# One spread stream of weight conversions in a fused attention and SwiGLU kernel

## The chip, the cores and the metric

The kernel runs on one core of one Trainium2 chip. The time is the device time of one execution in microseconds. A core has five engines that take their instructions in program order, each from its own queue, and wait for one another through semaphores: PE (TensorE, matrix multiply), DVE (VectorE), ACT (ScalarE), POOL (GpSimd) and SP, which here only issues DMAs. ACT issues DMAs too. PE writes to PSUM, which has eight banks of 2 KB a partition; other engines must empty a bank before PE can use it again.

## The reference

Rotary attention over 4 batches, 8 heads, 576 tokens and a head size of 64, and then a SwiGLU layer on the 2304 tokens of 512 values:

```python
attn = np.exp(scores - np.max(scores, axis=-1, keepdims=True))
attn = attn / (np.sum(attn, axis=-1, keepdims=True) + 1e-09)
x = np.matmul(attn, v).transpose(0, 2, 1, 3).reshape(2304, 512)
g = x @ w_gate                       # w_gate, w_val: 512 x 1536, w_out: 1536 x 512
silu = g * (1.0 / (1.0 + np.exp(-g)))
out = (silu * (x @ w_val) @ w_out).astype(np.float32)
```

Queries, keys and values are 32-bit floats; the weights come as 64-bit floats.

## The kernel before

Every 32-bit operand of a matmul is split into a high part `h` and a low part `l`, and a product is three matmuls: h·h, h·l, l·h. `split` makes the two parts: ACT casts the high part, and POOL or DVE subtracts it for the low one (both at line 674). A 64-bit weight is first made into a 32-bit one (`bits`, lines 720 to 726): a load of 512 KB into one of two `raw` buffers, one ACT operation (L720, the absolute value, "the sign bit" of the change), then six DVE operations (L721 to L726) of 128x512, in an `aux` PSUM bank.

The work after the attention has four stages. Tokens stand in two halves of 1152, each in three tiles of 384.

**Ordinary units** (`plain`): two blocks of 128 of the 1536 hidden columns are done as plain products, 2 blocks x 6 token tiles = 12 units u0 to u11 (`UNITS`) of 24 matmuls. `mm` writes to two of six PSUM banks; `ev` empties them on ACT (L766 Silu, L767 copy) and stores both results to DRAM, to `hf` for the first seven groups of 128 tokens (`FT = 7`) and to `ht` for the other eleven. So unit n+3 on PE waits for `ev` of unit n. Between the units stand: `xlate` (L662 to L666), which makes the second half's tokens ready, 4 chunks for each of two tiles (DVE add, DVE multiply, two ACT casts, DVE subtract, in sequence); `mix` and `forms2`, which make the token sums (T1, T0, T2) that the next stage multiplies; and the conversion of its first weights.

**Strassen passes**: the other ten blocks in ten passes s = 0 to 9 (gate and value in turn) through a seven-product scheme (`PROD`). A pass is three units q (token pairs p = 1, 2, 0), each of seven products of six matmuls. ACT copies the products k = 0 and 2 out of PSUM, DVE adds the five others, POOL makes two further sums after products 3 and 4 (L789). While pass s runs, `bits` converts the weights of pass s+2, `sums` (POOL) and two `split`s make the form `W0` or `W1` of pass s+1. The table `at(s, q, k, ...)` in `strassen` says after which product each of these stands in the program; `dq` is the list of conversion steps handed out after products. In gate passes ACT also applies Silu (L825) and issues the stores of the finished unit; in value passes SP issues them.

**First output part** (`finish`, first loop, `fdown`): for each of the 12 hidden blocks f, seven groups of 128 tokens times the output weights: 21 matmuls of 128x512. `fload` (SP) reads the block's gate and value, 896 KB, into one of two `HF` buffers, DVE multiplies them (L854), ACT casts `fh`, POOL subtracts `fl`; the output weight of block f+4 is converted (`obits`) and split (`Oh` on ACT, `Ol` on POOL).

**Second output part** (second loop, `down`): for the other eleven groups, 36 matmuls of 128x512 each.

All engines' order is the program's. Every DMA carries one of eight semaphores in turn, whichever queue issues it; a DMA whose semaphore is still held by an earlier one waits for that one's landing, and the instructions behind it in its queue wait too.

Of the kernel before, what the change touches and what calls it, by code (L numbers as in the profile page):

```python
# [52 lines left out]
    st=3,  # L53
# [461 lines left out]
FT = 7  # L515
# [3 lines left out]
class Moe:  # L519
# [50 lines left out]
    def open_early(self, ctx):  # L570
        def pool(name, bufs):
            return ctx.enter_context(self.tc.tile_pool(name=name, bufs=bufs, reuse_waits="tile", side="right"))
        one = pool("m_one", 1)
        self.Wb[1] = self.wbuf(one, 1)
        self.slot["raw0"] = pool("m_raw0", 1)
        self.s_p = pool("m_s", 3)
# [16 lines left out]
    def open_mid(self, ctx):  # L593
        def pool(name, bufs, **kw):
            return ctx.enter_context(self.tc.tile_pool(name=name, bufs=bufs, reuse_waits="tile", side="right", **kw))
        one = pool("m_mid", 1)
        self.wform(one, 1)
        self.own(one, "HF1", [128, 2, FT * 128], FP32)
        self.c_p = pool("m_cp", 2)
# [76 lines left out]
    def forms(self, p, c, Z, e, le):  # L676
# [8 lines left out]
        return ops, self.split(le, *(t[:, :, c] for t in self.T[p]), Z)  # L685
# [76 lines left out]
    def ev(self, f, s, t, ps):  # L762
        nc = self.nc
        sg = self.s_p.tile([128, BK], FP32, name="sv")
        v = self.s_p.tile([128, BK], FP32, name="sv")
# [5 lines left out]
    def keep(self, i, f, o, x, q):  # L771
        n = x.shape[-1]
        m = min(max(FT * 128 - o, 0), n)
        d = q.dma_start
        if m:
            d(out=self.hd[0][i, f, :, o:o + m], in_=x[:, 0:m])
        if m < n:
            t = (o + m) // 128 - FT
            d(out=self.hd[1][i, t:t + (n - m) // 128, :, f, :].rearrange("t p q -> p t q"),
              in_=x[:, m:n].rearrange("p (t q) -> p t q", q=128))  # L780
# [54 lines left out]
    def of(self, f):  # L835
        if not self.OF:
# [9 lines left out]
    def fload(self, f):  # L846
        if f < 2:
            self.HF.append(self.again(("WF1", "HF1")[f], [128, 2, FT * 128], FP32, "HF"))
        self.nc.sync.dma_start(out=self.HF[f % 2], in_=self.hd[0][:, f].rearrange("i p q -> p i q"))

    def fsplit(self, f):
        hh, hl = self.fs[f] = [self.again(f"xa{(f + 1) % 3}{x}", [128, FT * 128], F32R, f"f{x}") for x in "hl"]
        g, v = self.HF[f % 2][:, 0], self.HF[f % 2][:, 1]
# [30 lines left out]
    def hload(self, t):  # L884
        if t < FT + 2:
            self.HG[t % 2] = self.again(f"T0{'lh'[t % 2]}", [128, 2, NFF, 128], FP32, "hg")
        self.nc.sync.dma_start(out=self.HG[t % 2], in_=self.hd[1][:, t - FT].rearrange("i p f q -> p i f q"))

    def hsplit(self, t):
# [3 lines left out]
        for z in range(0, NFF, 3):  # L893
            g, v = (G[:, i, z:z + 3] for i in range(2))
# [46 lines left out]
def attn_swiglu(ctx: ExitStack, tc: tile.TileContext, qk, vr, wg, wv, wo, tab, out):  # L941
# [4 lines left out]
    hd = (dr.tile([2, NFF, 128, FT * 128], FP32, name="hf"), dr.tile([2, 18 - FT, 128, NFF, 128], FP32, name="ht"))  # L946
# [143 lines left out]
    jobs = plain(moe, ps)  # L1090
# [3 lines left out]
    strassen(moe, jobs)  # L1094
# [3 lines left out]
    finish(moe)  # L1098
# [15 lines left out]

def plain(moe, ps):
    nc = moe.nc
    ve, po = nc.vector, nc.gpsimd
    J = [Conv(moe, 1 + s // 2, s % 2, s % 2) for s in range(10)]
    st = {}
# [5 lines left out]
    for half in range(2):  # L1125
        J[0].load(half)
    moe.yload(1)
    moe.rload(1, 1)
    moe.yload(2)
    moe.rload(1, 2, moe.R12)  # L1130
    for c in range(2):
        mix(1, c, moe.Z2[:, c])
    for u, x in enumerate(UNITS):
# [4 lines left out]
        if u < 2:  # L1138
            run(J[0].bits(u, ve))
            J[1].load(u)  # L1140
        elif u < 6:
            for c in range(2):
                moe.xlate(2 * u % 4 + c, u // 2)
        if u == 1:
            run(J[0].sums(po))
        if u in (2, 3):
            run(st[1, u - 2])
        if u == 3:
            run(J[0].split(0, po))
        if u == 4:  # L1150
            run(J[0].split(1, po))
        if u == 5:
            moe.tagain(2)
            ops, st[2] = moe.forms2(po, ve)
            run(ops)
        if u == 6:
            run(J[1].bits(0, ve))
            J[2].load(0)
        if u == 7:
            run(st[2])  # L1160
            moe.tagain(0)
            mix(0, 0, moe.again("raw0", [128, 4, BK], FP32, "Z"))
            mix(0, 1, moe.rz())
        if u == 8:
            run(J[1].bits(1, ve))
            J[2].load(1)
        if u == 10:
            run(st[0, 0])
        if u == 11:
            run(st[0, 1])  # L1170
    return J
# [5 lines left out]
def strassen(moe, J):  # L1177
# [3 lines left out]

    def bits(s):
        ops = []
        for h in range(2):
            ops += J[s + 2].bits(h, ve) if s < 8 else moe.obits(2 * (s - 8) + h)
            ops.append((lambda h=h: J[s + 3].load(h)) if s < 7 else (lambda h=h: moe.oload(2 * (s - 7) + h)))
        return ops
# [4 lines left out]
    for s in range(9):  # L1192
# [5 lines left out]
        at(s, 0, 4, lambda s=s: run(J[s + 1].sums(po)))  # L1198
        at(s, 1, 2, hi)
        at(s, 1, 4, lo[0])  # L1200
        at(s, 2, 4, lo[1])
# [5 lines left out]
    for s in range(10):  # L1207
        fp, i = 1 + s // 2, s % 2
        dq = bits(s)
# [7 lines left out]
    for f in (2, 3):  # L1217
# [3 lines left out]
def finish(moe):  # L1221
    for f in range(NFF):
        if f + 2 < NFF:
# [46 lines left out]
```

## Time and profile before

| | us |
|---|---|
| three runs: lowest, median, highest | 787.62, 792.21, 792.47 |
| the profiled execution | 788.58 |
| its span, first to last instruction | 786.8 |

| busy in the span | PE | DVE | ACT | POOL |
|---|---|---|---|---|
| us | 719.0 | 552.9 | 406.1 | 469.5 |

Busy time is a mean over stages of different kinds, so each stage is read by itself: what PE waits for in it, and what stood on the chain of work that ended last. Starts are in us from the beginning of the span. PEclk is the clock granted to PE, 1.00 being the full 2.4 GHz.

### The profile page before, as it was taken

How to read it: one execution, taken by the hardware profiler on the slowest of the kernel's cores; microseconds unless marked ns; L12 is line 12 of the kernel's file. 1: busy time of each engine (PE TensorE's matmuls, PEld its weight loads, DVE VectorE, ACT ScalarE, POOL GpSimd, SP SyncE). 2: the span in 40 equal slices, each digit the busy share in tenths (PEclk: the TensorE clock that was granted, in tenths of full speed). 3: DMA queues.
4: the chain of work that ended last, by engine and by line, in shares of the span. 5: the costliest groups of instructions: out<-in, count | busy, mean ns of one | idle time of the engine just before them, and what ended most of it. 6: DMA issues, size and time to landing. Idle time of an engine off the chain costs nothing.

```text
span 786.8 us, 12626 instructions
## 1 busy us (share of the span) xinstructions
PE 719.0 (91%) x4356; PEld 670.1 (85%) x4356; DVE 552.9 (70%) x891; ACT 406.1 (52%) x878; POOL 469.5 (60%) x466
## 2 busy tenths in 40 slices
PE   7799999999999999686989899898998977899997
PEld 6699999999999989586889899898998855678887
DVE  4899888888888885565757566575656877745541
ACT  2689888888988863443531434314343223243331
POOL 5796989999899578369456464564655745400000
PEclk9999999999999999789889999999999999999999
DMA  5888698888888957924343454534447756676761
GB/s 150 219 205 219 180 249 219 217 217 219 210 211 215 226 172 179 226 69 134 93 148 113 129 151 134 170 108 135 147 134 238 250 201 222 253 264 213 228 218 41
DMA packets 103824, 144.11 MB, mean 183 GB/s; under 512 B 17728, under 2 KB 75088, under 8 KB 103760
## 3 DMA queue, kind: packets, MB, share of 16 engines
q1 hardware_dynamic: 77968, 125.71, 55.6%
q10 hardware_dynamic: 25792, 17.59, 7.3%
q8 instruction: 35, 0.57, 0.3%
q14 instruction: 29, 0.24, 0.1%
HBM read 76.61 MB, written 42.54 MB: 151 GB/s over the span
## 4 chain that ended last, share of the span: by engine, by line
PE 57%; POOL 11%; DVE 10%; DMA 8%; ACT 7%; issue 6%; ACTq 1%; SPq 1%; POOLq 0%; DVEq 0%
PE ch L801 18%; PE ch L908 12%; PE pv L476 9%; PE sc L360 8%; PE tr L436 6%; POOL fl L674 2%; DVE nmt L375 2%; DMA hf<-sv 2%; POOL W1l L674 1%; PE tr L299 1%; PE ch L758 1%; POOL Z L680 1%; POOL W0l L674 1%; ACT E L393 1%; POOL R L680 1%
## 5 line engine op out<-in xcount | busy, mean ns | idle before, releaser
L375 DVE TENSOR_REDUCE nmt<-sc 128x1 f32<-128x576 f32 x144 | 107.8, 750 | 21.1 <-PE sc L360 19.8
L393 ACT ACTIVATE E<-sc,nmt 128x576 f32<-128x576 f32 x128 | 97.2, 759 | 9.5 <-DVE nmt L375 8.6
L789 POOL TENSOR_TENSOR u<-u,z 128x384 f32<-128x384 f32 x30 | 30.4, 1014 | 102.7 <-DVE sg L789 88.5
L436 PE MATMUL tr<-ident,E 128*128 128x128 f32 x512 | 77.2, 274 | 0.6 <-DVE N L322 0.6
L360 PE MATMUL sc<-QK 128*128 128x288 f32 x248 | 61.5, 329 | 3.4 <-DMA QK<-N 2.0
L436 PEld LDWEIGHTS tr<-ident,E 128*128 128x128 f32 x512 | 61.6, 141 | 2.5 <-PE tr L299 1.3
L224 POOL TENSOR_TENSOR t<-X,tabs 128x256 f32<-128x256 f32 (+1 forms) x90 | 51.8, 596 | 15.5 <-DVE rot L228 6.8
L804 ACT COPY c<-ch 128x384 f32<-128x384 f32 x30 | 14.4, 479 | 78.1 <-PE ch L801 78.1
L360 PE MATMUL sc<-N,QZ 128*128 128x288 f32 x248 | 53.6, 298 | 1.1 <-DMA QZ<-N 1.1
L908 PE MATMUL ch<-Oh,hh 128*128 128x512 f32 (+1 forms) x144 | 54.0, 375 | 0.1
L908 PE MATMUL ch<-Oh,hl 128*128 128x512 f32 (+1 forms) x144 | 53.9, 374 | 0.0
L908 PE MATMUL ch<-Ol,hh 128*128 128x512 f32 (+1 forms) x144 | 53.8, 374 | 0.0
L437 ACT CAST ET2h<-tr 128x512 fp32r<-128x512 f32 x80 | 47.0, 587 | 12.5 <-PE tr L436 12.5
L438 DVE TENSOR_TENSOR ET2l<-tr,ET2h 128x512 fp32r<-128x512 f32 x80 | 52.9, 681 | 0.5 <-ACT ET2h L437 0.5
L721 DVE TENSOR_SCALAR aux<-aux 128x512 f32<-128x512 f32 x32 | 22.3, 696 | 40.8 <-ACT aux L720 40.6
L228 POOL TENSOR_TENSOR rot<-rot,t 128x512 f32<-128x512 f32 (+1 forms) x45 | 45.7, 1016 | 3.5
L789 DVE TENSOR_TENSOR sg<-ch,u 128x384 f32<-128x384 f32 x60 | 33.3, 554 | 19.8 <-PE ch L801 19.3
L438 DVE TENSOR_TENSOR ET1l<-tr,ET1h 128x512 fp32r<-128x512 f32 x64 | 42.7, 684 | 6.3 <-ACT ET1h L437 6.2
L674 ACT CAST hh<-hg 128x384 fp32r<-128x384 f32 x44 | 22.6, 514 | 47.1 <-DVE hg L895 46.3
L674 DVE TENSOR_TENSOR hl<-hg,hh 128x384 fp32r<-128x384 f32 x44 | 25.8, 587 | 29.8 <-ACT hh L674 29.8
L437 ACT CAST ET1h<-tr 128x512 fp32r<-128x512 f32 x64 | 36.4, 597 | 18.0 <-PE tr L436 14.8
L227 POOL TENSOR_TENSOR rot<-X,tabs 128x512 f32<-128x512 f32 (+1 forms) x45 | 45.6, 1014 | 0.0
(400 smaller groups left out, 2463.9 us busy)
## 6 DMA issues: line engine op xcount, KB each, us to landing
QK<-N SPq DMA_DIRECT2D x62, 288.0 KB, 4.8
hg<-ht SPq DMA_DIRECT2D x11, 1536.0 KB, 7.8
HF<-hf SPq DMA_DIRECT2D x12, 896.0 KB, 5.6
X<-in_qk_dram SPq DMA_DIRECT2D x15, 576.0 KB, 6.5
yd<-Y SPq DMA_DIRECT2D x31, 256.0 KB, 3.8
Xab<-yd SPq DMA_DIRECT2D x32, 192.0 KB, 6.1
raw<-in_moe_w_out_dram SPq DMA_DIRECT2D x12, 512.0 KB, 3.4
raw<-in_moe_w_gate_dram SPq DMA_DIRECT2D x11, 512.0 KB, 4.1
```

What stands on the lines that cost most here:

```text
L224: ins = e.tensor_tensor(out=sel(t2, u), in0=sel(x, w), in1=tb(Sn, u), op=ALU.mult)
L360: nc.tensor.matmul(ps[:, g, 0:288], l, rr[:, o + g * 288:o + (g + 1) * 288], start=(x == 0), stop=(x == len(terms) - 1))
L375: nc.vector.tensor_reduce(out=nmcol, in_=ps[:, :, 0:288], axis=AX.XY, op=ALU.max, negate=True)
L393: nc.scalar.activation(out=E.rearrange("p (a b) -> p a b", a=2), in_=ps[:, :, 0:288], func=ACTF.Exp, bias=nmcol, scale=1.0, accum_out=self ...
L436: nc.tensor.transpose(ps[:, c], E[:, o + c * 128:o + (c + 1) * 128], self.ident)
L437: nc.scalar.copy(dst[0], src)
L438: nc.vector.tensor_tensor(out=dst[1], in0=src, in1=r32(dst[0]), op=ALU.subtract)
L476: nc.tensor.matmul(st["ps"][:, 0:w], VS[:, sl, :], t, start=(x == 0), stop=(x == last))
L674: return [lambda: self.nc.scalar.copy(h, f), lambda: le.tensor_tensor(out=l, in0=f, in1=r32(h), op=ALU.subtract)]
L789: add = lambda e, out, in0, in1: e.tensor_tensor(out=out, in0=in0, in1=in1, op=ALU.add)
L801: nc.tensor.matmul(acc, l[:, w, c * 128:(c + 1) * 128], r[:, c], start=(n == 0), stop=(n == 5))
L908: self.nc.tensor.matmul(ps, l[:, f], r[:, z], start=(n == 0), stop=(n == 3 * NFF - 1))
```

## The change

The conversions become one list of jobs (`Stream`): the 20 halves of gate and value weights and the 12 output weights, in the order of their use, with the output weights 4, 5 and 6 put in after the weights of passes 4, 6 and 8 (into a new buffer `OX`). `take(n)` gives the steps of n jobs; after the fourth of a job's six DVE steps it puts the ACT operation of the **next** job (`sign`), and after the last one the load of the job after that (`load`). A pass takes one to three jobs and spreads their steps evenly over its 21 products. In `finish` the five output weights that are left (7 to 11) are converted in iterations 0 to 4, each with `sign` at the start of its iteration.

In the passes, `split` of the next pass moves up: the casts from after product (1, 2) to (1, 0), the two subtractions from (1, 4) and (2, 4) to (1, 1) and (1, 4), written as (unit, product).

In `plain`, four jobs are converted in the first four units in place of two; `xlate` moves from u2 to u5 to u4 to u7; the second token tile's loads move behind u1; `forms2` runs on DVE and not on POOL; the T0 sums start at u3 on POOL.

The DRAM buffers hold gate and value side by side: `hf` as [f, 128, 7, 2, 128] and `ht` as [t, 128, f, 2, 128]. So an ordinary unit is one store (two where the border between `hf` and `ht` runs through it) in place of two or four, `fload` and `hload` read one piece per partition of twice the length, and a Strassen store to `hf` writes pieces of 512 bytes where it wrote up to 3 KB. All Strassen stores are issued by SP.

```diff
+class Stream:
+    def take(self, n, ahead=True):
+        out = []
+        for x in range(n):
+            for k in range(6):
+                out.append(lambda k=k: self.ops[0][k]())
+                if k == 3 and (ahead or x + 1 < n):
+                    out.append(self.sign)
+            out.append(lambda: self.ops.pop(0))
+            out.append(self.load)
+        return out
...
     def ev(self, f, s, t, ps):
-        nc.scalar.activation(out=sg, in_=ps[0], func=ACTF.Silu)
-        nc.scalar.copy(v, ps[1])
-        for i, x in enumerate((sg, v)):
-            self.keep(i, f, s * SG + t * BK, x, nc.scalar)
+        sv = self.ld_p.tile([128, 2, BK], FP32, name="Xab").rearrange("p a q -> p (a q)")
...
+        self.keep(f, 9 * s + 3 * t, sv.rearrange("p t i q -> p t (i q)"), slice(0, 2), nc.scalar)
...
-            self.keep(i, 2 * fp + j, 2 * p * BK, sg[j].rearrange("p j q -> p (j q)"), (self.nc.scalar, self.nc.sync)[i])
+            self.keep(2 * fp + j, 6 * p, sg[j].rearrange("p j (t q) -> p (j t) q", q=128), slice(i, i + 1), self.nc.sync)
...
     for u, x in enumerate(UNITS):
-        if u < 2:
-            run(J[0].bits(u, ve))
-            J[1].load(u)
-        elif u < 6:
-            for c in range(2):
-                moe.xlate(2 * u % 4 + c, u // 2)
+        if u < 4:
+            run(S.take(1, u < 3))
         if u == 1:
             run(J[0].sums(po))
+            moe.yload(2)
+            moe.rload(1, 2, moe.R12)
+        if 4 <= u < 8:
+            for c in range(2):
+                moe.xlate(2 * u % 4 + c, u // 2 - 1)
...
-            ops, st[2] = moe.forms2(po, ve)
+            ops, st[2] = moe.forms2(ve, ve)
...
-        at(s, 1, 2, hi)
-        at(s, 1, 4, lo[0])
-        at(s, 2, 4, lo[1])
+        at(s, 1, 0, hi)
+        at(s, 1, 1, lo[0])
+        at(s, 1, 4, lo[1])
...
-                run(dq, {0: 2, 2: 2, 5: 1}.get(k, 0))
-        run(dq)
+                g += 1
+                run(dq, g * m // 21 - (m - len(dq)))
...
     for f in range(NFF):
+        if S.begun < len(S.jobs):
+            S.sign()
...
+        if S.ops:
+            run(S.take(1, False))
         if f + 4 < NFF:
-            run(moe.obits(f + 4))
             run(moe.osplit(f + 4))
-            if f + 6 < NFF:
-                moe.oload(f + 6)
         moe.fdown(f)
```

POOL in pass 0, before. The `u` and `sg` rows are the sums after products 3 and 4 of the units q = 0, 1, 2; `W1l` are the two low parts of the weights of pass 1.

```order
L789 TENSOR_TENSOR u<-u,z_5000 128x384
L789 TENSOR_TENSOR sg<-sg,z_5000 128x384
L928 TENSOR_TENSOR WF_4442<-WF_4442 128x256
L929 TENSOR_TENSOR WF_4442<-WF_4442 128x256
L930 TENSOR_TENSOR WF_4442<-WF_4442 128x256
L931 TENSOR_TENSOR WF_4442<-WF_4442 128x256
L789 TENSOR_TENSOR u<-u,z_5072 128x384
L789 TENSOR_TENSOR sg<-sg,z_5072 128x384
L674 TENSOR_TENSOR W1l<-WF_4442,W1h 128x1024
L789 TENSOR_TENSOR u<-u,z_5150 128x384
L789 TENSOR_TENSOR sg<-sg,z_5150 128x384
L674 TENSOR_TENSOR W1l<-WF_4442,W1h 128x1024
```

The same place in the change (the four `sums` of this one pass stand earlier, in the ordinary units).

```order
L786 TENSOR_TENSOR u<-u,z_4985 128x384
L786 TENSOR_TENSOR sg<-sg,z_4985 128x384
L674 TENSOR_TENSOR W1l<-WF_4439,W1h 128x1024
L786 TENSOR_TENSOR u<-u,z_5051 128x384
L786 TENSOR_TENSOR sg<-sg,z_5051 128x384
L674 TENSOR_TENSOR W1l<-WF_4439,W1h 128x1024
L786 TENSOR_TENSOR u<-u,z_5128 128x384
L786 TENSOR_TENSOR sg<-sg,z_5128 128x384
```

Both low parts stand one unit, seven products, earlier: the second one behind the sums of q = 1, not of q = 2.

ACT in the ordinary units u2 and u3, before: `sv` are the results, `xa2h` and `T0h` what `xlate` makes.

```order
L720 ACTIVATE aux<-raw 128x512
L766 ACTIVATE sv<-ch 128x384
L767 COPY sv<-ch 128x384
L776 DMA hf<-sv 128x128
L779 DMA ht<-sv 128x2x128
L776 DMA hf<-sv 128x128
L779 DMA ht<-sv 128x2x128
L664 CAST xa2h<-aux 128x384
L665 COPY T0h<-aux 128x384
L664 CAST xa2h<-aux 128x384
L665 COPY T0h<-aux 128x384
L674 CAST T1h<-T0l 128x4x384
```

The same place in the change; the two L720 rows are those of the third and the fourth job, and `Xab` is the buffer of the results.

```order
L720 ACTIVATE aux<-raw 128x512
L766 ACTIVATE Xab<-ch 128x3x128
L767 COPY Xab<-ch 128x3x128
L774 DMA hf<-Xab 128x256
L777 DMA ht<-Xab 128x2x256
L720 ACTIVATE aux<-raw 128x512
L674 CAST T1h<-T0l 128x4x384
```

Two of four stores and the four casts of `xlate` have left this place, and the absolute value of the third job now stands ahead of the Silu of u2, that of the fourth ahead of the Silu of u3.

ACT in `finish`, before: `fh` belongs to block f+2, L720 and `Oh` to the output weight f+4.

```order
L674 CAST fh<-HF 128x896
L720 ACTIVATE aux<-raw 128x512
L674 CAST Oh<-OF 128x512
L674 CAST fh<-HF 128x896
L720 ACTIVATE aux<-raw 128x512
```

The same place in the change, iterations 0 to 1 and 4 to 5:

```order
L720 ACTIVATE aux<-raw 128x512
L674 CAST fh<-HF 128x896
L674 CAST Oh<-OX 128x512
L720 ACTIVATE aux<-raw 128x512
L674 CAST fh<-HF 128x896
L674 CAST Oh<-OX 128x512
...
L674 CAST fh<-HF 128x896
L674 CAST Oh<-OF 128x512
L674 CAST fh<-HF 128x896
L674 CAST Oh<-OF 128x512
```

L720 comes first in its iteration and belongs to a weight that is split three iterations later; from iteration 5 on there is none. `Oh` takes a weight that was converted in an earlier iteration or pass.

## Rows read from the trace of the kernel before

**Rows 1.** Stretch, us, busy of PE PEld DVE ACT POOL, PEclk, DMA, GB/s
```profile
289.00:360.60 71.60, 60.62 (x314) 58.36 (x313) 43.97 (x61) 29.66 (x54) 46.51 (x33) 0.90 0.60 155
360.60:615.30 254.70, 229.11 (x1252) 225.09 (x1251) 161.57 (x274) 87.18 (x136) 143.56 (x125) 0.95 0.46 142
615.30:691.00 75.70, 63.54 (x264) 47.78 (x262) 55.71 (x72) 23.19 (x35) 39.86 (x23) 1.00 0.60 221
```
**Rows 2.** What PE waited for, 280 to 361 us: total, times, longest
```profile
PE ch L758 <- ACT sv L766: 10.7, 5, 4.0
```
**Rows 3.** The same, 361 to 616 us
```profile
PE ch L801 <- POOL W1l L674: 15.3, 5, 3.2
...
PE ch L801 <- POOL W0l L674: 2.4, 4, 0.6
```
**Rows 4.** The same, 615 to 691 us
```profile
PE ch L864 <- POOL fl L674: 11.1, 8, 1.4
```
**Rows 5.** The chain that ended last, in pass 0: start, us, what
```profile
394.50 0.96 POOL sg L789
395.46 2.31 POOL W1l L674
```
**Rows 6.** PE in order of time: two matmuls 92 apart, pass 9
```profile
600.83 0.34 PE L801 MATMUL ch<-xa1h,W1l 128*128 128x384 f32 x1
...
616.78 0.34 PE L801 MATMUL ch<-xb0l,W1h 128*128 128x384 f32 x1
```
**Rows 7.** The chain that ended last: the second output part
```profile
691.00 91.79 PE ch L908 x432
```
**Rows 8.** The chain that ended last, in the first output part
```profile
620.08 8.10 DMA HF<-hf
...
658.70 2.04 POOL fl L674
```
**Rows 9.** DVE in order, first output part; in brackets idle before
```profile
638.38 0.70 DVE L721 TENSOR_SCALAR aux<-aux 128x512 f32<-128x512 f32 x1 [1.58 <-ACT aux L720]
...
642.64 1.08 DVE L854 TENSOR_TENSOR HF<-HF 128x896 f32<-128x896 f32 x1
```
**Rows 10.** DMA issues 640 to 672 us: count, KB, us to landing
```profile
HF<-hf SPq DMA_DIRECT2D x5, 896.0 KB, 5.4
```
**Rows 11.** DMA issues 380 to 600 us
```profile
raw<-in_moe_w_val_dram SPq DMA_DIRECT2D x8, 512.0 KB, 3.4
```
**Rows 12.** DMA issues 300 to 330 us
```profile
raw<-in_moe_w_val_dram SPq DMA_DIRECT2D x2, 512.0 KB, 7.5
```
**Rows 13.** As rows 1: the loaded part of the ordinary units
```profile
303.00:330.00 27.00, 22.68 (x114) 22.04 (x112) 16.16 (x24) 7.92 (x17) 16.14 (x15) 0.87 1.09 265
```
**Rows 14.** ACT in order of time, ordinary units
```profile
322.25 0.49 ACT L767 COPY sv<-ch 128x384 f32<-128x384 f32 x1
325.25 1.50 ACTq L776 DMA_DIRECT2D hf<-sv  x2
```
**Rows 15.** DVE in order of time, ordinary units
```profile
316.35 0.57 DVE L663 TENSOR_TENSOR aux<-aux,R 128x384 f32<-128x384 f32 x1 [3.61 <-DMA R<-rd]
...
333.30 2.73 DVE L662 TENSOR_TENSOR aux<-T0h,T2h 128x384 f32<-128x384 f32 x1
...
338.03 0.56 DVE L662 TENSOR_TENSOR aux<-T0h,T2h 128x384 f32<-128x384 f32 x1
...
340.59 0.55 DVE L662 TENSOR_TENSOR aux<-T0h,T2h 128x384 f32<-128x384 f32 x1
```
**Rows 16.** POOL in order of time, at the second row of rows 15
```profile
332.61 3.00 POOL L674 TENSOR_TENSOR W0l<-WF,W0h 128x1024 fp32r<-128x1024 f32 x1 [12.92 <-ACT W0h L674]
```
**Rows 17.** PE in order: first matmul of pass 0's second unit
```profile
377.60 0.69 PE L801 MATMUL ch<-xa2h,W0h 128*128 128x384 f32 x1 [0.19 <-DVE u L789]
```
**Rows 18.** DVE's groups in the passes, by shape: busy us, mean ns
```profile
L789 DVE TENSOR_TENSOR sg<-ch,u 128x384 f32<-128x384 f32 x59 | 32.7, 555 | 19.8 <-PE ch L801 19.3
...
L725 DVE SCALAR_TENSOR_TENSOR aux<-raw,aux 128x512 f32<-128x512 uint32 x21 | 14.5, 691 | 0.4
```

More of the change, by code (lines that the diff above doesn't have):

```diff
@@ L597, in open_mid @@
         self.wform(one, 1)
-        self.own(one, "HF1", [128, 2, FT * 128], FP32)
+        self.own(one, "HF1", [128, FT, 2, 128], FP32)
+        self.OX = self.own(one, "OX", [128, NX, DM], FP32)
         self.c_p = pool("m_cp", 2)
@@ L1089, in attn_swiglu @@
     moe.open_aux(xctx, 2)
-    jobs = plain(moe, ps)
+    J, S = plain(moe, ps)
     mctx.close()
@@ L1093, in attn_swiglu @@
     moe.open_mid(mctx)
-    strassen(moe, jobs)
+    strassen(moe, J, S)
     xctx.close()
@@ L1112, with __init__, load, sign @@
          (0, 1, 1), (1, 1, 1), (0, 1, 2), (1, 1, 2)]
+class Stream:
+    def __init__(self, moe, jobs):
+        self.jobs = jobs
+        self.ops, self.loaded, self.begun, self.done = [], 0, 0, 0
+    def load(self):
+        if self.loaded < len(self.jobs):
+            self.jobs[self.loaded][0]()
+            self.loaded += 1
+    def sign(self):
+        if self.begun < len(self.jobs):
+            ops = self.jobs[self.begun][1]()
+            self.begun += 1
+            ops[0]()
+            self.ops.append(ops[1:])
+    def take(self, n, ahead=True):
[8 more added lines that the diff above has]
+        return out
 def plain(moe, ps):
@@ L1118, in plain, with job @@
     J = [Conv(moe, 1 + s // 2, s % 2, s % 2) for s in range(10)]
+    jobs = []
+    def job(kind, x, h=0):
+        if kind == "w":
+            jobs.append((lambda: J[x].load(h), lambda: J[x].bits(h, ve)))
+        else:
+            jobs.append((lambda: moe.oload(x), lambda: moe.obits(x)))
+    for s in range(10):
+        for h in range(2):
+            job("w", s, h)
+        if s in (4, 6, 8):
+            job("o", 2 + s // 2)
+    for f in (0, 1, 2, 3, 7, 8, 9, 10, 11):
+        job("o", f)
+    S = Stream(moe, jobs)
     st = {}
@@ L1123, in mix @@
         run(ops)
-    for half in range(2):
-        J[0].load(half)
+    S.load()
+    S.load()
     moe.yload(1)
     moe.rload(1, 1)
-    moe.yload(2)
-    moe.rload(1, 2, moe.R12)
+    S.sign()
     for c in range(2):
@@ L1149, in plain, with strassen @@
             run(J[0].split(0, po))
+            mix(0, 0, moe.again("raw0", [128, 4, BK], FP32, "Z"))
         if u == 4:
             run(J[0].split(1, po))
+        if 4 <= u < 8:
+            for c in range(2):
+                moe.xlate(2 * u % 4 + c, u // 2 - 1)
         if u == 5:
+            mix(0, 1, moe.rz())
+        if u == 7:
             moe.tagain(2)
-            ops, st[2] = moe.forms2(po, ve)
+            ops, st[2] = moe.forms2(ve, ve)
             run(ops)
[L1156 to L1159, printed above, removed]
+            run(J[1].sums(po))
+        if u == 8:
             run(st[2])
             moe.tagain(0)
[L1162 to L1166, printed above, removed]
+        if u in (9, 10):
+            run(moe.split(ve, *(t[:, :, u - 9] for t in moe.T[0]), st[0, u - 9]))
         if u == 10:
[L1168 to L1171, printed above, removed]
+            S.sign()
+            run(S.take(1))
+    return J, S
 ORDER = (1, 2, 0)
-def strassen(moe, J):
+def strassen(moe, J, S):
     nc = moe.nc
@@ L1208, in strassen @@
         fp, i = 1 + s // 2, s % 2
-        dq = bits(s)
+        n = {0: 1, 2: 3, 4: 3, 6: 3}.get(s, 2)
+        dq = S.take(n, s < 9)
+        m, g = len(dq), 0
         for q, p in enumerate(ORDER):
```

57 lines of the change are left out of this document (27 added, 30 removed).

## The prediction

> **What bounds the kernel now.** I read the page's share of busy time first, then the busy time by stretch, the PE waits of each stretch, the chain that ended last, and single engines in order of time where a wait stood out. PE is busy 719.0 of 786.8 us, so only its waits and its clock can be won. The attention's order is the same on every engine, and PE's order is the same everywhere: the matmuls stay. The second output part is bare PE: 432 matmuls in 91.79 us with no other engine in the chain [rows 7]; counted by width they are 396 full 512-column ones, 0.2318 us each. Nothing there moves. Three stretches remain, 289.0 to 360.6, 360.6 to 615.3 and 615.3 to 691.0 [rows 1]:
>
> - Ordinary units: PE waits 10.7 us for `sv`, in five waits, the longest 4.0 [rows 2].
> - Passes: 15.3 us for `W1l` in five waits and 2.4 for `W0l` in four [rows 3], at a granted clock of 0.95 [rows 1].
> - First output part: 11.1 us for `fl` in eight waits [rows 4], at full clock.
>
> The sum is made against the profiled execution's own 788.58 us. That lies 3.6 below the median of the three runs (792.21) and near the lowest (787.62).
>
> **Passes: −25 us (bounds −28 and −15).** 92 matmuls of pass 9 take 616.78 − 600.83 = 15.95 us, 0.1734 each, with no wait between [rows 6]. From the second unit of pass 0, at 377.60 [rows 17], to the first output part at 617.1 (the last row of [rows 6] and its 0.34) there are 29 units of 42 = 1218 matmuls: 211.2 us bare, 239.5 measured, 28.3 lost. 17.7 of these are the waits of [rows 3]; the other 10.6 is time at the lower of the two clock levels (1.2, not 2.4 GHz), which the stretch's 0.95 shows and which follows the long waits.
>
> In a gate pass the second `W1l` stands on POOL behind the sums of the unit q = 2: sum until 395.46, then the low part, 2.31 us, and PE wants it at once [rows 5]. So each wait is one such operation (15.3 / 5 = 3.1 with its surroundings). The change puts it seven products earlier: 42 × 0.1734 = 7.3 us, against a wait of 3.1, leaves 4 us. The casts ahead of it move too, to (1, 0); the first low part then waits for them and for POOL's `sums` of up to 2 us behind (0, 4), inside the same margin. The `W0l` waits of 0.6 go the same way. No wait, no fall of the clock: I book 25 of 28.3.
>
> What the even stream costs: before, a pass had two jobs; now it has one to three, 22 in all. In one with three, DVE has 15 evictions × 0.555 + 18 conversion operations × 0.691 [rows 18] = 20.8 us, against a pass of 126 × 0.1734 = 21.9. DVE is at 95% in three passes, 76% in the others (12 operations, 16.6 us). Six PSUM banks cover a late eviction by some 5 us. ACT's absolute value now stands between the copies of products and waits for a raw load that was issued half a job earlier: 21.9 / 3 / 2 = 3.65 us in the three-job passes, 5.5 in the others, where before's load landed after 3.4 [rows 11]; between ends of 3.4 and 7.5 (under heavy traffic, [rows 12]) I take 3.4, since the stretch moves 142 GB/s, not 265 [rows 1, 13]. 7.5 would make ACT 3.9 us late per job, under the banks' 5. If a third of the waits came back so, the term would be −15. The stores that leave ACT for SP cost nothing on PE: SP only waits.
>
> **First output part: −9 us (bounds −12 and −5).** 12 blocks of 21 matmuls are 252 × 0.2318 = 58.4 us; measured are 691.0 − 617.1 = 73.9. In every iteration DVE stands 1.58 us waiting for ACT's L720 and then does seven operations; the next L721 comes 645.30 − 638.38 = 6.92 us after the last one (the first is [rows 9]; six such periods follow alike), and `Ol` and `fl` (2.04, [rows 8]) come behind it. The change issues L720 at the iteration's start, so the 1.58 goes, and five iterations convert where eight did. What is then late, block by block from 617.1: block 3 still waits for its `HF` load, which took 8.10 us to 628.2 [rows 8]; multiply 1.08, cast 0.95, `fl` 2.04 and hand-overs put it at +16. Blocks 4 to 7 follow DVE: six operations at 0.73 (with the 0.03 between) and the multiply of 1.08, up to 1.6 with strided operands, 5.9 each: block 7 starts at +39.6. From there the two `HF` buffers are the limit: load 5.4 [rows 10], multiply, cast, `fl` and hand-over 4.8, 10.2 per two blocks, 5.1 each, against PE's 4.87. Four such blocks and the last block's 4.87: +64.9. The gain is 9.0. With PE bare after block 3 it would be +59.8 and some hand-overs, −12; with the `HF` loads at the 8.10 of the first one, 6.45 per block from block 7, −5.
>
> **Ordinary units: −2 us (bounds −9 and +4).** Moved here: four jobs in four units, `xlate` two units later, `forms2` to DVE, T0 earlier. For: before, DVE stood 3.61 us until 316.3 for an `R` load [rows 15], with casts ahead of the Silu on ACT; that goes. Against: the transfers run at 265 GB/s with all DMA engines busy (share 1.09, [rows 13]), so order decides. The raw load of the fourth job (0.52 MB, 2.0 us) now stands in the same train, lands near 316.8, and its absolute value stands ahead of a Silu: a new wait of some 3.5 us near u5, and the longest wait of before, 4.0, shrinks for it. The `T2` load then lands behind two raw loads, near 327.7 where before a store issue stood until 325.25 behind it (the copy ahead of it had ended at 322.74, [rows 14]). That store's 1.5 us and the Silu and copy behind it reach 331 to 332; eight `xlate` chunks at 340.59 − 338.03 = 2.56 us [rows 15] add 20.5, to 352.5; four DVE operations of `forms2` of about 0.9, a cast and a low part follow, 7 us: the passes start at 359.5, 1.1 sooner. Pass 0's first unit held 377.60 − 360.6 − 7.3 = 9.7 us of waits; with POOL freed of `forms2` and `sums` 3.5 of it go: second unit at 373, −4.6.
>
> The cover that could fail is shown by one row: L662 at 333.30 took 2.73 us where its likes take 0.56 [rows 15], and POOL's `W0l` ran from 332.61 for 3.00 [rows 16]; both ended within 0.5 us. Now all eight L662 and four `forms2` operations run beside POOL's long chain. I take half of the gain, 375.5, between 373 and the 378 to 380 of twelve late operations. Taken beyond these, −9 is most of the 10.7 of `sv` waits gone, and +4 the twelve operations all late (13 us) with two thirds of it covered or regained.
>
> The Trainium skill (page "SBUF — State Buffer", section "SBUF: two separate sides") says that DVE and GpSimd share one port pair as an exclusive lock held for the whole instruction, and that a DVE operation with two SBUF inputs against a GpSimd one that reads SBUF is such a case. By that rule every L662 and `forms2` operation that meets a running POOL operation waits to its end, and the term is about +2, not −2. The row at 333.30 agrees with it; the rows here do not show whether those of 0.56 met a POOL operation.
>
> **The sum.** −25 − 9 − 2 = −36: 752.6 as a profile, 754 as a median, some 1.4 above, since the three runs lie from 1 below to 4 above the profile.
>
> **Rivals.**
> - *DVE is held by POOL in all of the ordinary units.* Twelve operations lose half of 2.2 us each, some 13 on the chain, half of it covered by PE's units: the term is +2 in place of −2, and POOL's own low parts come late, so that one `W1l` wait of 3 stays: 754 + 4 + 3 = 761 (758 to 768). For it: the one row. Against: 338.03 and 340.59 run at 0.56.
> - *Raw loads come late in the passes.* SP now has all stores and loads of a pass in one line; if a load lands 6 to 7 us after issue, ACT and DVE lose the slack and PE waits 0.5 to 1 in each of the 22 jobs: +11 to +22, 765 to 776. Against: 3.4 [rows 11].
> - *The low part is not what PE waits for.* Should the second `W1l` be late for another reason (its `sums` or casts), the change would not do what it says; the passes lose their 25, the rest gives −11: 779 as a median.
> - *Slower.* The same line on SP, longer: a store waits for its unit's end, the raw load waits behind it, the absolute value holds ACT's copies, and PE's banks stay full. It takes a load that lands over 3.65 + 5 = 8.7 us after its step; from 1.7 us beyond that (10.4) in 22 jobs, 38 us, all of the gain is gone; at 11 it is 51 us, 805. The longest landing in these rows is 7.5 [rows 12].
>
> **How the numbers follow.** The forecast (744 to 762 by itself) has 0.60, the port rival 0.15, late loads 0.10, low parts unmoved 0.06, a gain near my lower bounds (below 744) 0.05, slower 0.04. 740 to 772 leaves out the unmoved and the slower case, a third of the late loads and half of the gains below 744, 0.16. About 1% is what a measurement of this kernel can tell from no change, 784.3 to 800.1 around the median; faster than that holds all cases but the slow one and half of "unmoved": 0.93, within 0.03, slower 0.04.
>
> **What would show it.** In the changed profile: no `W1l` wait above 1 us among PE's waits and a clock near 1.00 in the passes, 212 to 217 us from second unit to first output part (the step fails if 230 or more); 65 us for the first output part, its L721 without idle time before it; a new wait for `sv` of some 3.5 us near 315 with an absolute value as its releaser; L662 near 0.56 or near 2.7; the second unit of pass 0 between 373 and 380. The forecast is wrong above all if DVE at 95% makes PE wait in passes 2, 4 and 6, or if raw loads land after more than 5 us there.

## The result and the profile after

| | before | after |
|---|---|---|
| median us (four runs each) | 789.91 | 752.08 |
| lowest to highest | 786.11 to 792.47 | 751.81 to 752.31 |
| the profiled execution | 788.58 | 752.31 |

The ratio is 0.9525, 95% interval 0.9477 to 0.9572: 4.75% faster. The forecast was 754, with 740 to 772 as its range. So the sum was right to 2 us. Its three terms were not: two were too small and one had the wrong sign. Times are medians; one execution, 2427.95 us in the run with the stores alone, was slow for a reason that nothing here shows, and is left out.

The busy time by stretch of the changed kernel, cut where the stages meet (columns as [rows 1]): from the first ordinary matmul to the second unit of pass 0, from there to the first output part, the first output part, the second.

```profile
290.20:381.90 91.70, 70.74 (x354) 65.02 (x352) 62.06 (x78) 35.22 (x63) 50.58 (x41) 0.91 0.49 136
381.90:593.40 211.50, 211.41 (x1219) 211.41 (x1220) 158.28 (x282) 80.50 (x131) 130.95 (x113) 1.00 0.59 175
593.40:654.60 61.20, 58.64 (x253) 46.77 (x251) 40.24 (x51) 20.94 (x32) 38.92 (x22) 1.00 0.65 238
654.60:750.50 95.90, 91.77 (x432) 76.31 (x432) 41.94 (x81) 29.90 (x59) 0.00 (x0) 1.00 0.59 198
```

The second row is the point of the change: PE is busy in 211.41 of 211.50 us, at full clock. The same stretches of the kernel before are 88.4 (first ordinary matmul at 289.25 to 377.60), 239.5, 73.9 and 95.8 us. The account, by the starts of PE's first matmul in each:

| stretch | before | after | difference | forecast |
|---|---|---|---|---|
| attention, to the first ordinary matmul | 289.25 | 290.24 | +1.0 | 0 |
| ordinary units and first unit of pass 0 | 88.35 | 91.75 | +3.4 | −2 |
| passes, from the second unit of pass 0 | 239.5 | 211.4 | −28.1 | −25 |
| first output part | 73.9 | 61.3 | −12.6 | −9 |
| second output part | 95.8 | 95.8 | 0 | 0 |

The sum is −36.3, as the two profiled times are apart. The attention's +1.0 is no effect of the change: its order is the same, and over the kernels of this study its end lay anywhere from 288.6 to 290.6.

What PE waited for in the changed kernel (total, times, longest): the first two rows in 280 to 361 us, the next two in 361 to 600, the last in 600 to 680.

```profile
PE ch L758 <- ACT Xab L766: 10.3, 5, 3.5
PE ch L758 <- ACT xa2h L664: 3.7, 2, 2.7
```
```profile
PE ch L798 <- ACT Xab L766: 3.0, 3, 1.4
PE ch L798 <- DVE u L786: 1.6, 1, 1.6
```
```profile
PE ch L864 <- POOL fl L674: 1.6, 4, 0.5
```

No wait for `W1l` or `W0l` is left (15.3 and 2.4 in [rows 3]), and 1.6 us for `fl` where there were 11.1 [rows 4]. But the ordinary units have the 10 us of [rows 2] again, now for `Xab`, and a new wait for `xa2h`, a product of `xlate`.

### The profile page after: what moved, and what is told of

The parts are those of the page before. It is cut to its first block, busy times and chain, and to the rows that moved or that the text cites. A ratio compares the mean times of both kernels' runs of the same rounds, so it can differ in the third digit from the quotient of the medians.

```text
span 750.5 us, 12677 instructions
## 1 busy us (share of the span) xinstructions
PE 707.7 (94%) x4356; PEld 663.2 (88%) x4356; DVE 553.2 (74%) x895; ACT 402.9 (54%) x878; POOL 460.2 (61%) x462
## 4 chain that ended last, share of the span: by engine, by line
PE 64%; DVE 14%; DMA 11%; ACT 6%; issue 2%; POOL 2%; SPq 1%; ACTq 0%; DVEq 0%; POOLq 0%
PE ch L798 27%; PE ch L908 12%; PE pv L476 8%; PE sc L360 8%; PE tr L436 6%; DMA HF<-hf 2%; DVE nmt L375 2%; DVE aux L662 2%; PE tr L299 2%; DMA T0h<-yd 1%; ACT E L393 1%; DMA raw<-in_moe_w_gate_dram 1%; DMA T2h<-yd 1%; POOL fl L674 1%; DMA R<-rd 1%
## 5 line engine op out<-in xcount | busy, mean ns | idle before, releaser
L360 PEld LDWEIGHTS sc<-QK 128*128 128x128 f32 x248 | 38.6, 192 | 9.8 <-ACT E L393 4.8
L437 ACT CAST ET1h<-tr 128x512 fp32r<-128x512 f32 x64 | 36.4, 597 | 18.6 <-PE tr L436 15.3
```

What stands on the lines that cost most here:

```text
L360: nc.tensor.matmul(ps[:, g, 0:288], l, rr[:, o + g * 288:o + (g + 1) * 288], start=(x == 0), stop=(x == len(terms) - 1))
L437: nc.scalar.copy(dst[0], src)
```

## The experiments

Ratios are to the kernel before, timed beside each run, with the 95% interval in brackets. Beside the time stand the lengths of the stretches as in the table above, read from one profiled execution. The changed kernel and the run below with only its stores as before have the same stretches within 0.2 us, apart from the attention, and times of 752.08 and 750.69; so differences in time below some 1.5 us are read as nothing.

### Passes: which edit takes the waits away

**Low parts alone, on the kernel before.**

```diff
-        at(s, 1, 2, hi)
-        at(s, 1, 4, lo[0])
-        at(s, 2, 4, lo[1])
+        at(s, 1, 0, hi)
+        at(s, 1, 1, lo[0])
+        at(s, 1, 4, lo[1])
```

> The kernel before, with only the casts and low parts of the next pass moved up to (1, 0), (1, 1) and (1, 4). Theory: the place of the second low part alone makes the W1l waits and the falls of the clock behind them. Then the passes (from the second unit of pass 0 to the first output part) fall from 239.5 to 211 to 215 us, no W1l wait above 1 us is left, and the time is 25 to 28 below the kernel before: 761 to 766. Rival: the even stream of conversions is needed for it, since before's steps come in bunches after products 0 and 2: then waits stay, the passes take 225 or more, and the time is 776 or more.

Measured: 761.60 us, ratio 0.9656 (0.9612 to 0.9701), passes 212.8 us. No `W1l` wait is left. The three lines are enough. (The 212.8 are 1.4 above the changed kernel's 211.4. The granted clock is 0.99 from 377 to 600 us and 1.00 from 382: what is missing lies right behind a wait of 6.9 us in the first unit of pass 0, which this run shares with the kernel before.)

**The reverse: the changed kernel with the three lines as before.**

```diff
-        at(s, 1, 0, hi)
-        at(s, 1, 1, lo[0])
-        at(s, 1, 4, lo[1])
+        at(s, 1, 2, hi)
+        at(s, 1, 4, lo[0])
+        at(s, 2, 4, lo[1])
```

> The changed kernel, with only the casts and low parts back at (1, 2), (1, 4) and (2, 4). Theory: five W1l waits of about 3 us come back with the clock's 10 us, 752 + 25 to 28 = 777 to 780. Rival (the even stream takes the waits away by itself, because POOL and DVE are met by fewer things at once): 752 to 758.

Measured: 758.18 us, passes 219.8. The rival's number, 0.2 above its range, and some 19 us better than the theory. PE's waits in 360 to 617 us:

```profile
PE ch L798 <- POOL W1l L674: 3.2, 5, 0.6
PE ch L798 <- POOL W0l L674: 2.4, 4, 0.6
```

So the late place by itself makes a wait of 0.6 us a pass, as the value passes had always shown [rows 3], and not 3.1. (Nine such waits are 5.6 us; the passes are 8.4 longer than 211.4, at a clock of 1.00, so each costs some 0.3 beyond its length.) The other 2.5 us of a gate pass's wait come from something else that the change removes too. The kernel before shows it, in ACT's and then DVE's order of time in pass 2, a gate pass:

```profile
432.97 0.85 ACT L825 ACTIVATE sg<-sg 128x768 f32<-128x768 f32 x1
433.85 0.33 ACTq L776 DMA_DIRECT2D hf<-sg  x1
434.20 0.46 ACTq L779 DMA_DIRECT2D ht<-sg  x1
434.76 0.85 ACT L825 ACTIVATE sg<-sg 128x768 f32<-128x768 f32 x1 [0.94 <-DMA raw<-in_moe_w_val_dram]
435.64 0.33 ACTq L776 DMA_DIRECT2D hf<-sg  x1
436.00 0.46 ACTq L779 DMA_DIRECT2D ht<-sg  x1
436.51 2.00 ACT L674 CAST W1h<-WF 128x1024 fp32r<-128x1024 f32 x2 [0.90 <-ACT sg L825]
438.41 0.62 ACT L720 ACTIVATE aux<-raw 128x512 f32<-128x512 f32 x1
```
```profile
439.07 0.70 DVE L721 TENSOR_SCALAR aux<-aux 128x512 f32<-128x512 f32 x1 [2.87 <-ACT aux L720]
439.68 0.55 DVE L789 TENSOR_TENSOR sg<-ch,u 128x384 f32<-128x384 f32 x1
```

Silu, store, store, Silu, store, store, two casts, and only then the absolute value on which DVE stands: 2.87 us idle, with the evictions of finished products queued behind it. They run late through the rest of the pass, POOL's sums follow them, and the low part follows the sums. Two edits of the change could break this chain as well: the stores leave ACT, and the absolute value is taken ahead of time.

**The stores alone, on the kernel before.**

```diff
-            self.keep(..., (self.nc.scalar, self.nc.sync)[i])
+            self.keep(..., self.nc.sync)
```

> The kernel before, with one edit: the stores of the gate passes are issued by SP and not by ACT. Theory A: in the gate passes ACT stood in Silu, stores and the waits of the store issues (from 432.97 to 438.4 us in pass 2) ahead of the absolute value; DVE waited 2.87 us for that, its later sums came 3 us late, and so POOL's; without the stores the W1l waits fall from 3.1 to about 0.6 each, as in value passes, and the clock stays up: 768 to 775. Theory B (only the place of the low part counts): the W1l waits stay near 3 and the time is 786 or more.

Measured: 771.50 us (three executions, 768.90 to 774.21), ratio 0.9792 (0.9729 to 0.9855), passes 222.6. Theory A's number; that the time falls is clear of the noise, that it falls by 2% is not. The waits in 361 to 610 us:

```profile
PE ch L801 <- POOL W1l L674: 4.8, 5, 1.0
PE ch L801 <- POOL W0l L674: 2.4, 4, 0.6
```

**The changed kernel with the low parts and the stores both as before.**

```diff
-        at(s, 1, 0, hi)
-        at(s, 1, 1, lo[0])
-        at(s, 1, 4, lo[1])
+        at(s, 1, 2, hi)
+        at(s, 1, 4, lo[0])
+        at(s, 2, 4, lo[1])
...
-            self.keep(..., self.nc.sync)
+            self.keep(..., (self.nc.scalar, self.nc.sync)[i])
```

> The changed kernel with the low parts back at (2, 4), which alone gave 758.2 us, and besides with the gate passes' stores issued by ACT again. Theory A: the stores on ACT are what makes DVE and POOL late there, whatever the order of the conversions; the W1l waits grow from 0.6 to 2 or 3 and the time goes to 765 to 780. Theory B: with the absolute value taken early the stream keeps DVE fed although ACT is held, so the waits stay below 1 us: 757 to 761.

Measured: 762.70 us, between the two ranges, passes 221.7, with this wait in 361 to 600 us:

```profile
PE ch L798 <- POOL W1l L674: 5.1, 5, 1.3
```

Neither theory alone: the stores on ACT do make the waits longer (5.1 in all, not 3.2; 1.3 each behind the three passes with three jobs, 0.6 behind the other two), but with the new stream they do not become 15.3. Which part of the stream does this is not shown: the early absolute value is the likely one, but no run moves it alone in the passes.

**The changed kernel with only the stores as before.**

```diff
-            self.keep(..., self.nc.sync)
+            self.keep(..., (self.nc.scalar, self.nc.sync)[i])
```

> The changed kernel with one edit: the gate passes' stores are issued by ACT again, the low parts stay where the change put them. Theory: the low part's place gives 7.3 us of margin, more than the 3 us by which ACT's store issues make DVE and POOL late, so either edit alone takes the waits away: within 2 us of the changed kernel, 751 to 754, and no W1l wait above 0.5. Rival: ACT's issues hold up the casts of the high parts at (1, 0) and with them both low parts: 758 or more.

Measured: 750.69 us, ratio 0.9506 (0.9449 to 0.9563), the passes 211.4 and no wait for a low part: as in the changed kernel.

Together, the `W1l` wait per gate pass with the low part in its old place: 3.1 us with both old stores and old stream, 1.0 in the mean with either of them new, 0.6 with both new; with the low part moved it is none, whichever the stores are. Passes of 239.5, 222.6, 221.7, 219.8 and 211.4 us go with these. The clock adds to it in the kernel before alone: from 382 to 600 us it was granted 0.96 there, with waits of about 3 us, and 1.00 in the run with the stores alone and the one with the low parts and the stores as before, whose longest waits are 1.0 and 1.3.

### First output part: the absolute value or the three weights

**Eight weights converted there, as before, but each absolute value at the start of its iteration.**

```diff
...
-        if s in (4, 6, 8):
-            job("o", 2 + s // 2)
-    for f in (0, 1, 2, 3, 7, 8, 9, 10, 11):
+    for f in range(NFF):
...
-        n = {0: 1, 2: 3, 4: 3, 6: 3}.get(s, 2)
+        n = {0: 1}.get(s, 2)
```

(and the buffer `OX` goes)

> The changed kernel without the three output weights in the passes: eight are converted in the first output part, each with its absolute value still at the start of the iteration. Theory: what the first output part gained (73.9 to 61.3 us) came from the absolute value (1.58 us in each period); a period of DVE is then 6 x 0.73 + 1.09 = 5.5 us in eight iterations in place of five, so three more blocks lose 0.7 each: 63 to 65 us, the time 754 to 756. Rival: it came from the three weights; then the part takes 68 or more and the time is 759 or more.

Measured: 755.01 us, first output part 65.1.

**The same, and the absolute value just ahead of its conversion.**

```diff
     for f in range(NFF):
-        if S.begun < len(S.jobs):
-            S.sign()
...
-        if S.ops:
+        if S.begun < len(S.jobs):
+            S.sign()
             run(S.take(1, False))
```

> As the run before it, and the absolute value back behind the cast of its iteration, just ahead of its own conversion. Theory: the period is 6.92 us again, seven blocks lose 2.05 each to PE's 4.87: 72 to 74 us for the first output part, 762 to 765 in all. Rival (the three weights count, not the absolute value): no more than 1 us above the run before it.

Measured: 764.53 us, first output part 74.4, and DVE shows the idle time of [rows 9] again (in this kernel the lines lie one to three lower: L720 is L721 of before).

```profile
626.40 0.70 DVE L720 TENSOR_SCALAR aux<-aux 128x512 f32<-128x512 f32 x1 [1.58 <-ACT aux L719]
```

So the early absolute value gives 9.3 us (74.4 to 65.1) and the three weights 3.8 (65.1 to 61.3). That is 13.1, not 12.6: this last kernel takes 0.5 longer here than the kernel before, at a granted clock of 0.98 where that had 1.00, so up to some 1.5 of the 9.3 (0.02 of 74.4) may be the clock's. It has the new layout of `hf` and is no faster here than the kernel before, so no third cause of the gain shows.

### Ordinary units: what the change lost there

Six kernels have the change's order of the ordinary units (the changed one, and those above but for the two made from the kernel before); this stretch takes 90.5 to 92.3 us in them, so shorter ones stand out.

DVE's eight L662 of the changed kernel, four of them, and POOL at the same time:

```profile
333.95 2.74 DVE L662 TENSOR_TENSOR aux<-T0h,T2h 128x384 f32<-128x384 f32 x1
...
338.70 1.10 DVE L662 TENSOR_TENSOR aux<-T0h,T2h 128x384 f32<-128x384 f32 x1
...
344.96 2.65 DVE L662 TENSOR_TENSOR aux<-T0h,T2h 128x384 f32<-128x384 f32 x1
...
359.74 0.56 DVE L662 TENSOR_TENSOR aux<-T0h,T2h 128x384 f32<-128x384 f32 x1
```
```profile
333.27 3.00 POOL L674 TENSOR_TENSOR W0l<-WF,W0h 128x1024 fp32r<-128x1024 f32 x1 [13.22 <-ACT W0h L674]
...
338.36 1.01 POOL L680 TENSOR_TENSOR Z<-xm0h,xm0l 128x384 f32<-128x384 f32 x1
...
344.84 2.34 POOL L674 TENSOR_TENSOR W0l<-WF,W0h 128x1024 fp32r<-128x1024 f32 x1
```

Each long one ends 0.4 us after the POOL operation beside it: 336.69 after 336.27, 339.80 after 339.37, 347.61 after 347.18. The one at 359.74 met only the last 0.1 us of POOL's chain, which ended at 359.84, and took 0.56. All eight sum to 12.3 us, where eight of 0.56 are 4.5: 7.8 us lost on a chain on which PE then waits.

**T0 sums ahead of the low part.**

```diff
+        if u == 2:
+            mix(0, 0, moe.again("raw0", [128, 4, BK], FP32, "Z"))
         if u == 3:
             run(J[0].split(0, po))
-            mix(0, 0, moe.again("raw0", [128, 4, BK], FP32, "Z"))
```

> The changed kernel with one move: the first half of the T0 sums on POOL stands ahead of the first low part of W0, in the time when POOL stands still (320 to 333 us), and not behind it beside the xlate chunks. Theory (an addition on DVE with two SBUF inputs waits for the end of a running POOL operation): of the eight L662, those that met these sums (1.10 and 1.16 us at 338.7 and 341.8) take 0.56, the ones that meet the two low parts stay near 2.7 and move; xlate ends 1 to 3 us sooner and the time is 749 to 751. Rival (the long L662 come from transfers or from ACT): the durations stay, and the time is within 0.5 us of the changed kernel.

Measured: 749.46 us. The eight L662 take 9.2 us in all, not 12.3. The two that met the sums take 0.68 and 0.55 now, the first still 2.74. The fourth takes 0.56 and not 2.65, since both low parts now run one behind the other, up to 339.43, and it starts at 344.42. The stretch is 88.7 us, 3.0 less.

**W0's low parts on DVE.**

```diff
-            run(J[0].split(0, po))
+            run(J[0].split(0, ve))
...
-            run(J[0].split(1, po))
+            run(J[0].split(1, ve))
```

> The changed kernel with the two low parts of W0 in the ordinary units made by DVE and not by POOL. Theory (a running POOL operation holds up an addition on DVE with two SBUF inputs to its own end): the two L662 of 2.74 and 2.65 us become at most as long as the sums on POOL make them (0.56 to 1.6); DVE pays two subtractions of 128x1024, about 1.2 us each (1.76 for 128x1536): the eight xlate chunks take 1 to 3 us less from first to last than 28.4 us, the time is 749 to 752. Rival (those two are long for another reason, as a load or a wait on ACT): L662 stays near 2.7 at these places, and the chunks take longer than before by the two subtractions.

Measured: 748.49 us, the stretch 88.3. Some of DVE's L662 in order of time, and POOL's operations after its pause:

```profile
334.23 0.56 DVE L662 TENSOR_TENSOR aux<-T0h,T2h 128x384 f32<-128x384 f32 x1
...
341.91 0.56 DVE L662 TENSOR_TENSOR aux<-T0h,T2h 128x384 f32<-128x384 f32 x1
...
344.47 0.91 DVE L662 TENSOR_TENSOR aux<-T0h,T2h 128x384 f32<-128x384 f32 x1
...
347.39 2.15 DVE L662 TENSOR_TENSOR aux<-T0h,T2h 128x384 f32<-128x384 f32 x1
```
```profile
343.14 1.81 POOL L680 TENSOR_TENSOR R<-xa0h,xa0l 128x768 f32<-128x768 f32 x1 [15.45 <-DVE aux L663]
344.92 1.32 POOL L680 TENSOR_TENSOR R<-xm0h,xm0l 128x384 f32<-128x384 f32 x1
...
347.28 4.21 POOL L680 TENSOR_TENSOR R<-R 128x768 f32<-128x768 f32 x3
```

POOL stands still for 15.45 us, to 343.14, and the four L662 in that time take 0.56 each (the two between the rows shown, too). The next ones, beside the sums, take 0.91, 2.15 and 1.07. The eight chunks take 23.0 us, from 334.23 to 357.26: 5.4 less than 28.4, where 1 to 3 less were expected. The first half of the T0 sums, too, came before the chunks here (318.42 to 327.70), with no low part ahead of it on POOL. Same instruction, same place in the program: it is POOL's running beside them that makes them long.

**The ordinary units as in the kernel before.**

```diff
-        if u < 4:
-            run(S.take(1, u < 3))
+        if u in (0, 1, 6, 8):
+            S.sign()
+            run(S.take(1, False))
+        elif 2 <= u < 6:
+            for c in range(2):
+                moe.xlate(2 * u % 4 + c, u // 2)
...
-            ops, st[2] = moe.forms2(ve, ve)
+            ops, st[2] = moe.forms2(po, ve)
```

(and the second tile's loads ahead of the units, the T0 sums at u7, two jobs and the sums in pass 0)

> The changed kernel with the ordinary units ordered as in the kernel before: xlate in u2 to u5, third and fourth job in u6 and u8, forms2 on POOL, the T0 sums at u7; pass 0 then converts two jobs and makes its own four sums. Theory: the ordinary units of the change cost 3.4 us (from the first ordinary matmul to the second unit of pass 0 it took 91.75 us after, 88.35 before), so the time is 748 to 750, with the wait of 6.9 us in pass 0 back and the L662 of 2.7 us gone but one. Rival: pass 0 now carries two jobs and the sums besides the late T0 parts, and pays it back: 752 or more.

Measured: 748.40 us, the stretch 86.9, passes 213.0. The new order of the ordinary units is a loss: 4.8 us in its stretch, 3.7 in the whole time. The wait in pass 0 that the old order brings back is 7.4 us here; in the kernel before it was this one, in 361 to 616 us:

```profile
PE ch L801 <- ACT c L804: 6.9, 1, 6.9
```

**The two orders mixed:** as the last one, but `forms2` on DVE, the T0 sums on POOL at u2 and u4, the T0 parts at u9 and u10.

> A mixture of the two orders: loads, xlate and conversions of the ordinary units as in the kernel before (xlate in u2 to u5, third and fourth job in u6 and u8, so that no absolute value and no raw load stands ahead of the second tile's loads), but forms2 on DVE and the T0 sums early on POOL (u2 and u4, the T0 parts in u9 and u10). Theory: the waits for the third and fourth raw load (3.5 us) go, the wait of 6.9 us in pass 0 goes too, since POOL has no late T0 sums: 742 to 747. Rival: the transfers of the second tile bound the stretch whatever the order, and the late jobs on DVE hold up forms2's parts: 750 or more.

Measured: 740.33 us, below the range; ratio 0.9388 (0.9333 to 0.9442), the stretch 79.7. The wait of pass 0 is gone, and the stretch is 7.2 us shorter than in the run before this one: that is what `forms2` on DVE with the early T0 sums is worth. Against the changed kernel's 91.7 it is 12.0 shorter, which puts the loss on that order's early jobs, late loads and late `xlate` together. Left are, in 289 to 375 us,

```profile
PE ch L758 <- ACT Xab L766: 13.3, 5, 4.2
```

**xlate one unit later in it.**

```diff
-        if u in (0, 1, 6, 8):
+        if u in (0, 1, 7, 9):
...
-        elif 2 <= u < 6:
+        if 3 <= u < 7:
             for c in range(2):
-                moe.xlate(2 * u % 4 + c, u // 2)
+                moe.xlate(2 * (u - 1) % 4 + c, (u - 1) // 2)
```

(and `forms2` in u6)

> As the mixed order of the ordinary units (740.3 us), with xlate one unit later (u3 to u6), forms2 in u6 and the late jobs in u7 and u9. Theory: its waits at u6 and u7 (3.1 and 4.2 us) are for a Silu that stands on ACT behind the casts of xlate, which wait for the R load (landed 316.6) and T2l load (near 325.9); one unit later the Silu runs first, so the PE wait at u6 goes and the next ones shrink: 733 to 739. Rival (the landing of those loads bounds the stretch, whatever stands ahead of what): the waits only move to u7 and u8, 739.5 to 743.

Measured: 734.28 us, ratio 0.9296 (0.9240 to 0.9352), the stretch 75.0. The wait falls to this, over the same time:

```profile
PE ch L758 <- ACT Xab L766: 8.5, 6, 4.2
```

This is the best kernel of the study, 18 us below the changed one: the passes and output parts of the change (211.4 and 60.7 us), and ordinary units in neither of the two orders.

## Why the prediction was right, point by point

**The time was right, by errors that cancel.** Ordinary units +3.4 where −2 was forecast, passes −28.1 for −25, first output part −12.6 for −9. With the attention's +1.0 that is −36.3 against −36. That the errors leave 0.3 is luck.

**Passes.** The bare count, 1218 × 0.1734 = 211.2 us, was met to 0.2. The step "I book 25 of 28.3" kept 3 us for waits that would stay, and none did. DVE, put at 20.8 of 21.9 us in the three-job passes, was busy 18.35 of 21.86 in one of them (462.25 to 484.11, 84%), and never held PE up. Raw loads landed after medians of 3.3 to 3.9 us from 380 to 590 us, so the rival of late loads, and the slower case built on it, had nothing to stand on. Not all of the 10.6 us put to the clock were the clock's: the nine waits cost some 0.3 each beyond their length at full clock, as above, which is 2.8 of it.

The reason given was enough but not the only one. "So each wait is one such operation (15.3 / 5 = 3.1 with its surroundings)" was a false reading: the wait came near the low part's 2.31 by chance. The late place makes 0.6 of it; DVE's 2.87 us behind ACT made the sums late and cost most of the rest, as the run with the stores alone shows (1.0 left). "The stores that leave ACT for SP cost nothing on PE" is true of the changed kernel (750.69 with them back on ACT), but by itself that edit takes 16.9 us off the passes of the kernel before. The edits of the passes cover one another, so their gains do not add: the low parts alone take 26.7 us off the passes, the stores alone 16.9, the rest of the change without either 17.8, and all of them 28.1.

**First output part.** The mechanism was right and its parts were shown; three sizes were not, and the bound of −5 was mis-added (39.6 + 4 × 6.45 + 4.87 is 70.3 us, which is −3.6). Block 3 was put at +16 and did not wait at all: its `fl` ended at 607.85, +14.5, since its `HF` load landed 1 us sooner than the 8.10 of [rows 8] stood for. The DVE period was 5.4 to 5.6 us, not 5.9, as the multiply with strided operands takes 1.09 to 1.20 in these iterations and not up to 1.6:

```profile
609.00 1.09 DVE L854 TENSOR_TENSOR HF<-HF 128x896 f32<-128x896 f32 x1 [0.22 <-DMA HF<-hf]
610.00 0.69 DVE L721 TENSOR_SCALAR aux<-aux 128x512 f32<-128x512 f32 x1
...
614.60 1.09 DVE L854 TENSOR_TENSOR HF<-HF 128x896 f32<-128x896 f32 x1 [0.27 <-POOL Ol L674]
615.61 0.69 DVE L721 TENSOR_SCALAR aux<-aux 128x512 f32<-128x512 f32 x1
```

This is DVE in order of time: from one L721 to the next 5.61, with no wait for ACT. And the last four blocks do not wait for the two `HF` buffers: these turn at 5.1 us, as worked out (issues at 618.93 and 639.46, four apart), but their `fl` ended 0.1 to 0.8 us ahead of the matmul that reads them.

**Ordinary units.** The step that failed is "I take half of the gain": the chain was longer than even its late end. The new wait at u5 came with the forecast's 3.5 us, with the absolute value of the third job ahead of a Silu, where the fourth job was named. The absolute value of the fourth, at 323.51, waited 3.77 us for DVE and not for its load. PE, and ACT in order of time:

```profile
319.43 0.44 PE L758 MATMUL ch<-xa1h,w0h 128*128 128x384 f32 x1 [3.47 <-ACT Xab L766]
```
```profile
318.34 0.63 ACT L720 ACTIVATE aux<-raw 128x512 f32<-128x512 f32 x1 [12.97 <-DMA raw<-in_moe_w_val_dram]
318.90 0.47 ACT L766 ACTIVATE Xab<-ch 128x384 f32<-128x384 f32 x1
...
330.41 0.33 ACTq L774 DMA_DIRECT2D hf<-Xab  x1
330.77 1.47 ACT L674 CAST T1h<-T0l 128x1536 fp32r<-128x1536 f32 x1 [4.49 <-DMA T2l<-rd]
```

The `T2l` load, which the forecast calls the `T2` load, held ACT's store until 330.4, not 327.7: 5.2 us later than before's 325.25, where 2.4 were allowed for the two raw loads ahead of it. With them behind it (the mixed order) the same store is issued at 325.9. Then the eight chunks took 28.4 us (333.95 to 362.38) and not 20.5: 7.8 of it is DVE held by POOL. The passes started at 369.6 where 359.5 was worked out, and their second unit at 381.99, outside the 373 to 380 that were given as a sign; the eight L662 took not 0.56 or 2.7 but all lengths between as well.

The forecast gave this outcome, DVE held by POOL in all of the ordinary units and a term of +2, a chance of 0.15; the term was +3.4, and the wait for `W1l` that it added to this rival did not come. The Trainium skill (page "SBUF — State Buffer", section "SBUF: two separate sides") has the cause as an exclusive lock for a whole instruction. The traces bear it out (0.56 beside a still POOL, 2.74 beside a running one). One row of before showed it [rows 15, 16], and the two rows of 0.56 at 338.03 and 340.59 were put against it; but POOL stood still then, as its next row shows:

```profile
341.10 2.38 POOL L674 TENSOR_TENSOR W0l<-WF,W0h 128x1024 fp32r<-128x1024 f32 x1 [5.49 <-ACT W0h L674]
```

With POOL's chain laid beside all eight L662 of before, the hold would have been seen as the rule: the three that started beside a running POOL operation took 0.80 (at 318.32), 2.73 and 1.01 (at 344.69), the five others 0.55 to 0.56.

## What to carry to other kernels

A wait that is about as long as the operation it names need not be that operation's cost: look at when the operation's own inputs came, and whose idle time lies ahead of them, before an edit is priced; two edits that break the same chain are priced once. An instruction of one engine on which another engine's queue stands (here an absolute value on ACT, in front of six DVE steps) belongs well ahead of its use, and behind nothing that waits for a transfer. When work moves from POOL to DVE or beside it, lay the two engines' rows of the new order side by side and add, for every DVE operation with two SBUF inputs, the rest of the POOL operation that it meets.

## What the runs showed of the hardware

That a POOL operation holds up DVE so completely was not expected: an addition of two SBUF tiles took 0.56 us beside a still POOL and up to 2.74 beside a running one, ending 0.4 us after it. The multiply L663 between these, which takes one input from PSUM, took 0.56 to 0.57 throughout, in the same stretch and beside the same sums. Two pairs of rows speak for the other way too: in the changed kernel POOL's `W0l` at 333.27 took 3.00 us, the one at 344.84 2.34; the first had started while DVE's `T1l` (332.28, 1.76 long, two SBUF inputs) still ran, to 334.04. In the kernel before the two took 3.00 and 2.38, and the first, at 332.61, met `T1l` (331.62, 1.76 long) alike. No run changes this alone.
